# Fourteen four-quarter loads cut into 112 and 16 rows, and the early output rows written in five pieces

## The chip, the cores and the metric

The kernel runs on one core of a Trainium2 chip. The metric is the device time in microseconds of one execution; where several executions are given, the median counts. Lower is better.

## The reference

One decode step (one new token per batch entry, 8 entries, model width 448) through two layers. Each layer is attention over a long cache and then an MLP:

```python
def _A_ref(x, k_cache, v_cache, wq, wo):          # 16 query heads, 8 kv heads, 4096 keys, head width 256
    q = (x @ wq).reshape(B, 1, 16, 256) ...
    scores = einsum("bhqd,bhkd->bhqk", q, k) * 256 ** -0.5
    o = einsum("bhqk,bhkd->bhqd", softmax(scores), v)
    return o.reshape(B, 1, 16 * 256) @ wo
...
x = x + _A_ref(_layernorm(x), A_k_cache, A_v_cache, A_wq, A_wo)
x = x + _B_ref(_layernorm(x), B_w1, B_w2, B_w3, B_w4)
x = x + _A_ref(_layernorm(x), A_k_cache, A_v_cache, A_wq, A_wo)   # the same caches again
x = x + _B_ref(_layernorm(x), B_w1, B_w2, B_w3, B_w4)
```

The caches are bf16; K and V have 2 MB for each of the 64 pairs of batch entry and kv head, 256 MB together. Both layers read the same caches, but they don't fit on the chip, so most of them are read from HBM twice.

## The kernel before

**Tiles.** SBUF holds a pool `kv` of 30 slots called quarters, each 4096 bytes in all 128 partitions, 512 KB. One K or V tile of a head is four quarters: its 4096 keys are laid out as 128 rows of 32 keys, 16 KB each, so a load of a whole tile reads 128 contiguous rows of 16 KB and writes one row into each partition. Some quarters are kept from one layer's pass to the next (`KEEP_K`, `KEEP_V`), so the loads differ in size: one, two, three or four quarters.

**Order of the work.** The kernel records its operations with an engine, a duration, the keys that it reads and writes, and a priority (`Plan.op`). `Plan.schedule` then simulates all engines and fixes each engine's instruction order, and `Plan.synchronise` derives the semaphore waits. SP issues the loads in a fixed order of priority. When a load's turn comes, `next_kv` picks the free quarters, and `issue_kv` (L642 to L650) writes the DMA instruction at L648:

```python
slot_n[q] += 1
o.emit = lambda eng: eng.dma_start(dst, src)
o.dma = (slot_sem[q], 16 * slot_n[q])
```

Each quarter has a semaphore of its own, counted up by 16 per load; a reader waits for the count. Before the instruction SP waits until the last reader of the quarters, mostly a matmul (L1278, L1408), has finished. SP issues in order, so a load that waits for a quarter holds back those behind it.

**Counting TensorE's instructions.** The planner also models that TensorE's own instructions are fetched from memory in blocks of 128 matmul pairs (a weight load and a matmul): `fetched` counts them, and `pairs` in `schedule` is the number so far.

**The output.** The last results come in two parts. `with_first_results` finishes six batch entries early, in the step of entry `MLP_ROW`, and `result(6, 0)` (L1524) transposes them into `o_row`, six rows of 448 elements in six partitions, and writes them with one DMA at L1538. It is an SP instruction in the middle of the kv loads, placed by `OUT_AT`. The buffer `o_row` lies over `kh`, which later operations write again, and they wait for that DMA. The last two entries go out at the end, from L985, by SP and ACT, four rows each of `o_last`. SP's last instructions wait for the semaphores of the three writes.

The functions that the change touches:

Of the kernel before, what the change touches and what calls it, by code (L numbers as in the profile page):

```python
# [6 lines left out]
P = 128  # L7
B = 8
D = 448
# [14 lines left out]
HOLD = 2  # L24
MARGIN4, MARGIN2 = 6, 2
REP = 24
AT = (-4, -3, -2)
MLP_ROW, MLP_AT, MLP_TO = 5, 3, 7
G = D // 4
OUT_AT = 23.5  # L30
# [61 lines left out]
class Plan:  # L92
# [69 lines left out]
    def schedule(self):  # L162
# [26 lines left out]
        pairs, next_block = 32, 0.0  # L189
# [3 lines left out]
        n = 0  # L193
# [47 lines left out]
        while n < len(self.ops):  # L241
# [26 lines left out]
            if e == "sp":  # L268
                o = sp_next[sp_i]
                sp_i += 1  # L270
                if o.unit is not None:


                    _, m, q = kv_at
                    for x in range(m):
                        p = sp_next[sp_i - 1 + x]
                        p.unit.slot = q + x
                        if self.tenant[q + x] is not None:
                            o.deps[self.tenant[q + x]] = False
                        self.free_at[q + x] = 1e9  # L280
                        if x:
                            for s in p.succ:
                                del s.deps[p]
                                if o in s.deps:
                                    left[s] -= 1
                                else:
                                    s.deps[o] = True
                                    o.succ.append(s)
                            taken.add(p)
                            gone.add(p)  # L290
                            n += 1
                    sp_i += m - 1
                    self.issue_kv(o, m, q)
            else:
                while pend[e] and pend[e][0][0] <= t + 1e-9:
                    r, i, o = heapq.heappop(pend[e])
                    if o not in taken:
                        heapq.heappush(avail[e], (o.prio, i, o))
                while avail[e][0][2] in taken:
                    heapq.heappop(avail[e])  # L300
                o = heapq.heappop(avail[e])[2]
            if e == "pe" and self.filler and not quiet and t - free["pe"] > 0.1:
# [3 lines left out]
                while u + 0.22 <= t + 0.06:  # L306
# [18 lines left out]
                    while win < w:  # L325
# [5 lines left out]
                    u, pairs, next_block = self.fetched(u, f.dur[0] if warm else f.dur[1],  # L331
                                                        f.dur[3], pairs, next_block)
# [20 lines left out]
            else:  # L353
                d = o.dur
                if e == "pe":

                    w = int(t / self.WIN)
                    while win < w:
# [5 lines left out]
                    end, pairs, next_block = self.fetched(t, d[0] if warm else d[1], d[3],  # L364
                                                          pairs, next_block)
# [113 lines left out]
def bass_interleave_layers__gqa_block_cached__mixer_s_mlp__decode_kernel(  # L479
# [20 lines left out]
    plan = Plan()  # L500
# [62 lines left out]
    def over(name, shape, dt, at, skip=0):  # L563
        return nc.alloc_sbuf_tensor_at(name, shape, dt, offset=at.manual_sbuf_range[0] + skip)
# [11 lines left out]
    o_row = over("o_row", [B, D], bf, kh)  # L576
# [32 lines left out]
    s_out = nc.alloc_semaphore("s_out")  # L609
    s_outs = [nc.alloc_semaphore(f"s_out{i}") for i in range(2)]  # L610
    sems = {e: nc.alloc_semaphore(f"s_{e}") for e in ("pe", "dve", "act", "pool")}
    slot_sem = [nc.alloc_semaphore(f"s_slot{i}") for i in range(QUARTERS)]
    slot_n = [0] * QUARTERS

    def bcast(ap, shape, axis):

        dims = [list(x) for x in ap.ap]
        dims.insert(axis, [0, shape])
        return bass.AP(tensor=ap.tensor, offset=ap.offset, ap=dims)
# [19 lines left out]

    loads = [0]  # L640

    def issue_kv(o, n, q):  # L642

        (cache, b, h), u = o.unit.tile, o.unit.u
        src = cache[b, h].rearrange("(m s) d -> m (s d)", m=P)[:, u * 2048:(u + n) * 2048]
        dst = kv[:, q * 2048:(q + n) * 2048]
        slot_n[q] += 1
        o.emit = lambda eng: eng.dma_start(dst, src)  # L648
        o.dma = (slot_sem[q], 16 * slot_n[q])
        o.dur = ((n << 15) / 26.88e3 + 8 * 0.008) / FASTER + SHORT * (n < 3)  # L650

# [17 lines left out]
    KH = ["kh", ("khb", 0), ("khb", 1)]  # L669
# [18 lines left out]
    def const_c(v):  # L688
# [7 lines left out]
            wr=["sel"])  # L696
# [7 lines left out]
    for bank, key in [(psR, "R"), (psM, M)]:  # L704
        plan.op("dve", lambda v, bank=bank: v.memset(bank[:, :], 0.0), 0.5, "const",
                wr=["psM", ("row", 0), ("row", 1)], banks=[key])
# [7 lines left out]
    def dv(fn, dur=0.13, rd=(), wr=(), banks=(), name="chain", prio=None):  # L714
        if prio is None:
            prio = urge[0] + len(plan.ops)
        return plan.op("dve", fn, dur, name, rd=rd, wr=wr, banks=banks, prio=prio)
# [6 lines left out]
    def pe(fn, n, rd=(), wr=(), banks=(), name="chain", prio=None, width=20):  # L724

        if prio is None:
            prio = urge[0] + len(plan.ops)
        d = 0.06 + 0.026 * n
        return plan.op("pe", fn, (d, max(d, 0.06 + n * width / 1200), width * n, n), name, rd=rd, wr=wr, banks=banks, prio=prio)

    def mark(o):

        if where[0][1] != "psM":
            o.tbank = where[0][1][1]
# [370 lines left out]
    done = {}  # L1105
# [12 lines left out]
    def front(layer, b, h, prio=None):  # L1118
# [12 lines left out]
        def rhs(c):  # L1131
            a = at_q(layer, b, c) + 2 * h
            return qz[:, a:a + 2]
# [9 lines left out]
        def score(parts):  # L1143
            def sc(t):
                last = None
                for u, s, a in parts:
                    i = 8 * u + s


                    for c in range(2):  # L1150
                        last = t.matmul(ps[:, SB + 2 * i:SB + 2 * i + 2 * REP], a()[:, c:256:2],  # L1151
                                        bcast(rhs(c), REP, 1), start=(c == 0), stop=(c == 1))
                return last
            return sc

        def score_op(u, ss, where_of, keys):
            n = 2 * len(ss)
            return plan.op("pe", score([(u, s, lambda s=s: where_of(s)) for s in ss]),
                           (0.022 * n + 0.06, n * 2 * REP / 1200 + 0.01, n * 2 * REP, n), "sc",
                           rd=qk + keys, wr=[("sc", par, x) for x in range(u, 4)], banks=[bk],  # L1160
# [363 lines left out]
    def result(n, at):  # L1524

        ps, key, bk = where[0]

        def ot(t):
            last = None
            for kc in range(4):  # L1530
                w = P if kc < 3 else 64
                last = t.transpose(ps[0:n, :].bitcast(bf)[:, kc * P:kc * P + w],
                                   xoT[0:w, kc, at:at + n], ident_b[0:w, 0:w])
            return last
        pe(ot, 4, rd=[("xo", at), "ident_f"], wr=[key], banks=[bk])
        mark(dv(lambda v: v.tensor_copy(o_row[0:n, :], ps[0:n, :].bitcast(bf)[:, 0:D]), dur=0.5,
           rd=[key], wr=["o_row"] + KH, banks=[bk]))
        plan.op("sp", lambda eng: eng.dma_start(out[at:at + n, 0, :], o_row[0:n, :]), 0.1, "out",  # L1538
                rd=["o_row"] + KH, wr=[("done", n)],
                dma=(s_out, 16), prio=loads[0] + OUT_AT)  # L1540

    def mid(b, heads):

# [97 lines left out]

    def both(layer, b, heads, ahead=(), lag=1, AT=AT):


        tasks = []
        n = len(heads)
        for i in range(n + lag):
            if i < n:
                tasks.append(("f", layer, b, heads[i]))
            tasks += [("f",) + a for a, at in zip(ahead, AT[len(AT) - len(ahead):]) if at == i - n]  # L1650
            if i >= lag:
                tasks.append(("b", layer, b, heads[i - lag]))
        return tasks

    def with_first_results(k, b):

        if b != MLP_ROW:
            return run(k)
        run(k[:MLP_AT])
        urge[0] = 0  # L1660

        i = tcount[0] % NT
        where[0] = (psT[i], ("psT", i), ("T", i))
        held_banks.add(i)
        mlp(x3T[:, :, :], "x3all", B - 2, xoT[:, :, 0:B - 2], [("xo", 0), "x3all"])
        result(B - 2, 0)
        urge[0] = CH
        where[0] = (psM, "psM", M)
        run(k[MLP_AT:MLP_TO])
        held_banks.remove(i)  # L1670
        run(k[MLP_TO:])
# [11 lines left out]
    for b in range(B):  # L1683
# [16 lines left out]
        else:  # L1700
            k = both(1, b, l2_heads, [(1, b, h) for h in free_heads], AT=LAST_AT)
            for h, at in zip(l2_heads[-1:] + free_heads, BACKS):
# [28 lines left out]
    with nc.Block() as blk:  # L1731
        @blk.gpsimd
        def _(gp):
            plan.emit("pool", gp, sems)

        @blk.sync
        def _(eng):
            plan.emit("sp", eng, sems)
            for s in [s_out] + s_outs:
                eng.wait_ge(s, 16)  # L1740

        @blk.tensor
        def _(pe_):
            plan.emit("pe", pe_, sems)

        @blk.vector
        def _(v):
            plan.emit("dve", v, sems)

        @blk.scalar  # L1750
        def _(a):
            plan.emit("act", a, sems)
# [28 lines left out]
```

## Time and profile before

| | |
|---|---|
| time, median of 3 runs | 1073.85 us (1071.85 to 1077.86) |
| the profiled execution's own time | 1071.22 us |
| its span, first to last instruction | 1069.4 us |
| granted TensorE clock | 0.964 |
| TensorE matmul busy | 938.3 us (88%) |
| VectorE, ScalarE busy | 600.6 us (56%), 332.2 us (31%) |
| read from HBM | 434.18 MB, 406 GB/s over the span |
| kv loads of four quarters | 70 of K (22.6 us from issue to landing), 61 of V (18.5) |
| kv loads of one quarter | 168 of V (8.5 us), 26 of K (8.2) |

The page gives one profiled execution. Its slices show the busy share of each engine in tenths, and for DMA the mean busy share of the core's sixteen DMA engines. The time from issue to landing of a load includes the time that it stands in the queue behind earlier loads. The trace also has, for each DMA, one event for each part that lands, and each DMA packet with its queue, size and duration.

### The profile page before, as it was taken

The numbers are of one execution on the slowest core, as the hardware profiler recorded it, in microseconds if no ns is written. First come the engines' busy times: TensorE is split into PE (matmuls) and PEld (weight loads), VectorE is DVE, ScalarE is ACT, GpSimd is POOL, SyncE is SP. The second block draws the span as 40 slices with busy tenths as digits, with TensorE's granted clock in tenths as the row PEclk, the third lists the DMA queues.
The fourth block names the chain that finished last, engine by engine and source line by source line (L and its number), as shares of the span: only waits on it lengthen the run. The fifth ranks groups of instructions, "written<-read, shape, count | busy, mean of one in ns | idle before, by whom it ended". The sixth has DMA issues, their size and how long they took to land.

```text
span 1069.4 us, 34024 instructions
## 1 busy us (share of the span) xinstructions
PE 938.3 (88%) x15170; PEld 655.7 (61%) x15170; DVE 600.6 (56%) x1899; ACT 332.2 (31%) x926; POOL 99.6 (9%) x284
## 2 busy tenths in 40 slices
PE   5989899898989989898888878998899899898896
PEld 4556666565657656666565656766666676666664
DVE  4345455655556555565565655665555655666564
ACT  1234113341323403244132431334223432253141
POOL 0000010010100101001010100100010100111011
PEclk9899899999998999999999998999999989999997
DMA  9999999999999999999999999999999999999995
GB/s 364 408 427 423 409 398 426 427 421 400 415 424 426 421 398 410 427 425 419 395 422 425 426 410 375 426 426 424 403 400 423 425 405 379 416 423 419 373 423 235
DMA packets 56814, 436.39 MB, mean 408 GB/s; under 512 B 6094, under 2 KB 9308, under 8 KB 34652
## 3 DMA queue, kind: packets, MB, share of 16 engines
q1 hardware_dynamic: 56500, 433.84, 98.5%
q8 instruction: 119, 1.95, 0.7%
q10 hardware_dynamic: 168, 0.38, 0.1%
q14 instruction: 27, 0.22, 0.1%
HBM read 434.18 MB, written 0.01 MB: 406 GB/s over the span
## 4 chain that ended last, share of the span: by engine, by line
DMA 54%; PE 37%; DVE 6%; issue 2%; ACT 1%; SPq 0%; POOL 0%
DMA kv<-in_A_k_cache_dram 34%; DMA kv<-in_A_v_cache_dram 21%; PE psT L1512 12%; PE psP L1278 7%; PE psT L1408 4%; PE psM L1151 3%; PE psM L904 2%; PE psR L1342 2%; PE psP L1721 1%; PE psM L1068 1%; DVE oS L1306 1%; DVE oS L1304 1%; PE psM L920 1%; DVE kv L1443 1%; PE psP L1314 1%
## 5 line engine op out<-in xcount | busy, mean ns | idle before, releaser
L1512 PE MATMUL psT<-ident_f,kv 128*128 128x128 f32 x2752 | 379.5, 285 | 26.2 <-DMA kv<-in_A_k_cache_dram 24.7
L1512 PEld LDWEIGHTS psT<-ident_f,kv 128*128 128x128 f32 x2752 | 306.8, 144 | 107.7 <-issue 54.6
L1443 DVE COPY kv<-psT 128x512 f32<-128x512 f32 x384 | 262.5, 690 | 179.1 <-PE psT L1512 171.7
L1444 ACT COPY kv<-psT 128x512 f32<-128x512 f32 x336 | 195.9, 586 | 382.0 <-PE psT L1512 310.3
L1278 PE MATMUL psP<-kv,pT 128*2 128x256 bf16 x4032 | 165.4, 277 | 20.1 <-DMA kv<-in_A_v_cache_dram 16.6
L1408 PE MATMUL psT<-kv,qz 128*32 128x512 bf16 x1664 | 134.7, 397 | 6.1 <-DVE kv L1443 2.0
L1278 PEld LDWEIGHTS psP<-kv,pT 128*2 128x2 bf16 x4032 | 81.1, 82 | 59.2 <-DMA kv<-in_A_v_cache_dram 22.0
L1231 POOL PARTITION_ALL_REDUCE gm<-pm x128 | 45.4, 355 | 762.3 <-DVE pm L1229 759.8
L1241 ACT ACTIVATE pT<-sS,nb,fac 128x32 bf16<-128x32 bf16 x128 | 52.6, 417 | 123.2 <-DVE nb L1235 123.2
L1304 DVE CAST oS<-psP 128x256 bf16<-128x256 f32 x126 | 53.1, 422 | 40.6 <-PE psP L1278 39.3
L1245 POOL PARTITION_ALL_REDUCE Db<-rs x128 | 51.0, 398 | 188.9 <-ACT pT L1241 188.9
L1342 PE MATMUL psR<-wo_sb,oT 128*1 128x448 bf16 x444 | 61.0, 359 | 7.3 <-DVE oT L1321 3.5
L1314 PE MATMUL psP<-sel,oS 128*128 128x28 bf16 x504 | 32.8, 177 | 33.4 <-DVE oS L1306 30.9
L1423 DVE CAST sr<-psT 128x512 bf16<-128x512 f32 x60 | 41.5, 691 | 34.7 <-PE psT L1408 34.5
L1314 PEld LDWEIGHTS psP<-sel,oS 128*128 128x128 bf16 x504 | 23.3, 97 | 61.4 <-DVE oS L1306 57.1
L1408 PEld LDWEIGHTS psT<-kv,qz 128*32 128x32 bf16 x1664 | 34.3, 95 | 41.2 <-issue 12.3
L1241 ACT ACTIVATE pT<-sS,nb 128x32 bf16<-128x32 bf16 x128 | 40.7, 326 | 59.0 <-DVE nb L1235 59.0
L1306 DVE TENSOR_TENSOR oS<-psP,oS 128x256 bf16<-128x256 f32 x126 | 53.3, 423 | 2.9
L1721 PE MATMUL psP<-ident_f 128*128 128x256 bf16 x326 | 51.4, 283 | 0.0
L1224 DVE CAST sS<-psM 128x64 bf16<-128x64 f32 x128 | 28.1, 219 | 39.9 <-PE psM L1151 24.7
L1151 PE MATMUL psM<-qz,kv 128*128 128x48 bf16 x1344 | 45.2, 183 | 3.6 <-issue 2.1
L1151 PEld LDWEIGHTS psM<-qz,kv 128*128 128x128 bf16 x1344 | 38.9, 96 | 15.3 <-issue 5.1
(197 smaller groups left out, 805.3 us busy)
## 6 DMA issues: line engine op xcount, KB each, us to landing
kv<-in_A_k_cache_dram SPq DMA_DIRECT2D x70, 2048.0 KB, 22.6
kv<-in_A_v_cache_dram SPq DMA_DIRECT2D x61, 2048.0 KB, 18.5
kv<-in_A_v_cache_dram SPq DMA_DIRECT2D x168, 512.0 KB, 8.5
kv<-in_A_v_cache_dram SPq DMA_DIRECT2D x16, 1024.0 KB, 9.1
kv<-in_A_k_cache_dram SPq DMA_DIRECT2D x10, 1536.0 KB, 17.5
kv<-in_A_k_cache_dram SPq DMA_DIRECT2D x26, 512.0 KB, 8.2
kv<-in_A_k_cache_dram SPq DMA_DIRECT2D x8, 1024.0 KB, 9.6
kv<-in_A_v_cache_dram SPq DMA_DIRECT2D x4, 1536.0 KB, 10.0
```

Of the source, the lines that this page charges most:

```text
L1151: last = t.matmul(ps[:, SB + 2 * i:SB + 2 * i + 2 * REP], a()[:, c:256:2], bcast(rhs(c), REP, 1), start=(c == 0), stop=(c == 1))
L1241: return a.activation(pT[nr][:, :, :].rearrange("p i j -> p j i")[:, jj, :], sview[:, jj, :], ACT.Exp, bias=nb[nm][:, jj:jj + 1], scale=sc ...
L1278: last = t.matmul(ps[g4:g4 + 2, PV0:PV0 + DH], pT[nr][:, k, :], slot_ap(q, s * 256, 256), start=(i < 4), stop=(i >= 28), skip_group_check= ...
L1304: plan.op("dve", lambda v: v.tensor_copy(oS[:, 0, :], po), 0.36, "o", rd=[("pv", par, x) for x in range(4)], wr=["oS0"], banks=[bk], prio=hi)
L1306: plan.op("dve", lambda v: v.tensor_tensor(oS[:, 1, :], po, oS[:, 0, :], ALU.subtract), 0.36, "o", rd=["oS0"] + [("pv", par, x) for x in r ...
L1314: last = t.matmul(ps[:, PV1 + 2 * c:PV1 + 2 * c + 2 * ON], oS[:, w, c:DH:2], bcast(sel[:, :], ON, 1), start=(w == 0), stop=(w == 1))
L1342: last = t.matmul(psR[r:r + 1, 0:D], oT[no][:, i % 2, i // 2:i // 2 + 1], wo_sb[:, a:a + D], start=(k == 1 and i < 2), stop=(k == turn_at ...
L1408: last = t.matmul(psT[bank][32 * g:32 * g + 32, :], qz[:, a:a + 32], slot_ap(qs[g // 2], g % 2 * 1024, 1024)[:, c:1024:2], start=(half == ...
L1443: return e.tensor_copy(dst, psT[bank][:, :])
L1444: return e.copy(dst, psT[bank][:, :])
L1512: last = t.transpose(psT[bank][:, s * P:(s + 1) * P], src, ident_f[:, :])
L1721: return t.matmul(dst, ident_b, bcast(ident_b[:, 0:n // 4], 4, 1), start=True, stop=True)
```

## The change

When the planner reaches a load of four quarters, and TensorE's pairs so far have passed the next multiple of 1024, that load becomes two DMAs: rows 0 to 111, and rows 112 to 127 with the source written as eight groups of two rows. Both count on the same semaphore, and the reader waits for both. The six early output rows are written by five DMAs, cut by rows and columns, and the waits for them go from 16 to 80.

```diff
+SHARE, EVERY = 8, 1024
...
-                    self.issue_kv(o, m, q)
+                    self.issue_kv(o, m, q, pairs)
...
+    shifted = [0]
...
         slot_n[q] += 1
         o.emit = lambda eng: eng.dma_start(dst, src)
+        if n == 4 and pairs >= EVERY * (shifted[0] + 1):
+            shifted[0] += 1
+            slot_n[q] += 1
+
+            def two(eng):
+                eng.dma_start(dst[0:P - 16, :], src[0:P - 16, :]).then_inc(slot_sem[q], 16)
+                return eng.dma_start(dst[P - 16:P, :], src[P - 16:P, :].rearrange("(a m) x -> a m x", a=SHARE))
+            o.emit = two
         o.dma = (slot_sem[q], 16 * slot_n[q])
...
-        plan.op("sp", lambda eng: eng.dma_start(out[at:at + n, 0, :], o_row[0:n, :]), 0.1, "out",
-                rd=["o_row"] + KH, wr=[("done", n)],
-                dma=(s_out, 16), prio=loads[0] + OUT_AT)
+        pieces = [(0, 2, 0, 150), (2, n, 0, 150), (0, 3, 150, 298), (3, n, 150, 298), (0, n, 298, D)]
+
+        def write(eng):
+            for i, (r, r1, c, c1) in enumerate(pieces):
+                last = eng.dma_start(out[at + r:at + r1, 0, c:c1], o_row[r:r1, c:c1])
+                if i < len(pieces) - 1:
+                    last.then_inc(s_out, 16)
+            return last
+        plan.op("sp", write, 0.1, "out", rd=["o_row"] + KH, wr=[("done", n)],
+                dma=(s_out, 16 * len(pieces)), prio=loads[0] + OUT_AT)
...
-            for s in [s_out] + s_outs:
+            eng.wait_ge(s_out, 80)
+            for s in s_outs:
                 eng.wait_ge(s, 16)
```

In the built program there are 14 such pairs; the planner's order of instructions on each engine is otherwise the same.

More of the change, by code (lines that the diff above doesn't have):

```diff
@@ L640, in bass_interleave_layers__gqa_block_cached__mixer_s_mlp__decode_kernel, with issue_kv @@
     loads = [0]
-    def issue_kv(o, n, q):
+    shifted = [0]
+    def issue_kv(o, n, q, pairs):
         (cache, b, h), u = o.unit.tile, o.unit.u
```

## The prediction

> **What bounds the kernel now.** I read the clock first (0.964 granted, one core), then the page's slices and DMA queues, then the chain.
>
> ```profile
> span 1069.4 us, 34024 instructions
> ...
> DMA  9999999999999999999999999999999999999995
> GB/s 364 408 427 423 409 398 426 427 421 400 415 424 426 421 398 410 427 425 419 395 422 425 426 410 375 426 426 424 403 400 423 425 405 379 416 423 419 373 423 235
> ...
> q1 hardware_dynamic: 56500, 433.84, 98.5%
> q8 instruction: 119, 1.95, 0.7%
> ...
> DMA 54%; PE 37%; DVE 6%; issue 2%; ACT 1%; SPq 0%; POOL 0%
> ```
>
> The sixteen DMA engines are busy in every slice, SP's queue q1 alone takes 98.5% of them, and over half of the chain that ended last is transfers. TensorE is busy for 88% of the span and still waits for transfers. So a microsecond added to or taken from every DMA engine is nearly a microsecond of the end. Next, what paces the queue:
>
> ```profile
> SPq L648 <- PE psP L1278: 474.5, 139, 25.8
> SPq L648 <- PE psT L1408: 243.7, 49, 12.9
> ```
>
> SP spends 718 us in these two waits for a free quarter and then issues in bursts; a four-quarter load lands 18.5 to 22.6 us after its issue and needs 4.9 us to move, so three or four lie queued. SP's own time is no limit; the time on the DMA engines is.
>
> The last view is the rate by stretch (columns: stretch, its us, five engines' busy us, granted clock, DMA share, GB/s):
>
> ```profile
> 3.40:4.40 1.00, 0.00 (x0) 0.00 (x0) 0.07 (x1) 0.00 (x0) 0.00 (x0) 1.00 1.11 237
> 4.40:5.40 1.00, 0.29 (x6) 0.24 (x7) 0.18 (x1) 0.00 (x0) 0.00 (x0) 1.00 1.27 281
> 6.60:7.80 1.20, 0.00 (x0) 0.00 (x0) 1.06 (x9) 0.00 (x0) 0.00 (x0) 1.00 0.98 410
> 160.00:200.00 40.00, 35.80 (x472) 25.27 (x469) 22.69 (x61) 12.07 (x31) 3.01 (x8) 0.96 1.01 425
> ```
>
> From 3.4 to 5.4 us the only loads under way are those of 64 rows (wqx and w3x). All engines are busy (a share over 1 is packets side by side), yet they move 237 to 281 GB/s. The 128-row loads at 160 us move 425 with the same share. The packets say the same: a 4096-byte packet of the 64-row load has a median of 274.5 ns, a full-speed one 159. So which rows a DMA writes decides its rate, and not only how many engines share it.
>
> **Part 1: fourteen loads cut in two.** The built program of the change holds 14 pairs of a 112-row and a 16-row load of 16 KB rows; the other instructions stand in the same order on every engine. It removes nothing, and the bytes are the same.
>
> *Is work moved between DMA engines?* The design is plain: eight engines would take two of the last 16 rows each (7 + 2) and eight none (7). In this trace a load has as many landing events as it has rows where these are under 16 (eight for the 8-row x, six for the 6-row output, four for the 4-row ones) and sixteen for 128 rows. [...] But in the built program the source is one dimension of 16 rows: the step of `a` is twice the step of `m`, so the two were merged, and both sides are 16 rows of 8192 elements. I therefore expect sixteen engines with one row each, 7 + 1 = 8 as before, and nothing moved. [...]
>
> *Cost of the cut itself.* 14 more issues at about 0.4 us (1.24 us for the pair of loads at 2.88) are 5.6 us on SP, hidden behind its 718 us of waits; uncovered they would cost 0.4 us each. Behind each stands the next kv load, with the queue some 15 us deep. Semaphore packets: 14 more on each engine at 9 ns, 0.1 us.
>
> *Cost of other rows on the engines.* No 112-row and no 16-row load is in the trace; the nearest rows are the 128-row and the 64-row rate. The 112-row part (1.835 MB) takes 4.32 us at 425 GB/s and 7.74 at 237: 0 to 3.4 us more. The 16-row part (0.262 MB) takes 0.62 us at 425 and 1.11 at 237, 0.5 more; should a quarter of 64 rows mean a quarter of its rate, 4.4 us, 3.8 more. Below nothing neither can go without moved work. I take 1.1 us for the first (seven eighths of the rows are closer to 128 than to 64, but seven rows per engine no longer make equal groups of four) and 1.6 for the second, between 0.5 and 3.8, nearer to the row that exists. Together 2.7 us per load, between 0 and 7.2.
>
> 14 x 2.7 = 38 us of DMA time (0 to 101). Some is absorbed: in the eight stretches of small V loads (about 20 us each, 160 of 1069, 15%) SP's waits set the pace and not the engines, so I let 15% go: 32 us. What is late next is TensorE's transpose of the K load behind the pair (PE psT waits for in_A_k_cache_dram already).
>
> [...]
>
> **Part 2: the output in five pieces.** One issue of 0.31 us at 868.66 becomes five, so 1.2 us more on SP, and 18 packets of about 300 bytes in place of six (a 896-byte packet took 42 ns), under 0.3 us on the few engines that carry them. Behind the pieces the next kv loads wait:
>
> ```profile
> 868.66 0.31 SPq L1538 DMA_DIRECT2D out_dram<-o_row  x1
> 870.10 0.35 SPq L648 DMA_DIRECT2D kv<-in_A_v_cache_dram  x1
> 871.55 6.80 SPq L648 DMA_DIRECT2D kv<-in_A_k_cache_dram  x2
> ```
>
> The second of the loads at 871.55 waits for its quarter far longer than 1.2 us, so the delay is covered; without the cover it costs 1.2 us. The next writer of the same memory (the copy to kh at 890.1) is 16 us behind the landing at 874, and the final wait for 80 has been met since then. Nothing.
>
> **Sum.** 1071.22 us of the profiled execution (its span 1069.4 and 1.8 around it) + 32 = 1103. That execution is 2.6 us under the median of the runs, so the forecast for a median is 1073.85 + 32 = 1106.
>
> **The rivals.**
> *The work does move, and the end comes earlier* (1068). The eight engines that also carry the instruction fetches lag: at 25.2 us fifteen parts of a load land within 0.43 us and one 1.84 us after the first; at 79 us seven or eight lag by 1.5 to 2; before a stretch of small loads the spread is 4 to 5.4 us, then it shrinks because the early engines run dry. [...] A fetch of 16 KB takes 0.7% x 16 x 1069 / 119 = 1.0 us, 15 per late engine. If the 16 rows go to the eight light ones, each late engine is rid of 14 rows of 0.62 us, 8.6 us at most. The earliest engine runs dry by some 19 us in all over the eight stretches, others by less, so the light ones can take most of it before they set the end: about 6 us less. It decides if the pair's second load lands in eight parts and the unusual rows cost under 0.4 us per load. Against it stands the merged pattern. Chance 0.07.
> *Nothing moves and nothing collides*: the sixteen parts are as fast as before, because the neighbours in the queue fill the gaps. Then SP's and the packets' 0 to 2 us are all: 1075. For it: the 64-row loads are at the start, where the queue isn't yet deep. Against it: all engines were already busy there. Chance 0.15.
> *The slowest engine takes the whole blow each time.* A load counts as landed when its last part does; if the same engines share their rows' way in all 14 pairs, the delay per load is nearer to 5 us than to 2.7: 70 us, 1144. The fixed lag of the fetch engines shows that a lag persists over a whole stretch. Chance 0.15.
> *The work moves and the rows collide*: the fetch engines gain 0.6 us per pair and lose some 2, about 20 us, 1094. Chance 0.08.
>
> **The numbers.** My case (2.7 us per load, nothing moved; its own range 1084 to 1125) has the remaining 0.55. Half a per cent, 5.4 us, is about what a measurement of this kernel can tell from no change. Faster by more: the first rival, 0.07. Within it: 0.15. Slower: 0.55 + 0.15 + 0.08 = 0.78. The range must leave out no more than 2 in 10: from 1072, which drops the first rival and a little of the second, to 1136, which takes in the lower half of the third.
>
> **What would show it.** The DMA issues should list 14 groups' worth of 1792 KB and 256 KB loads. If I am right, 16 KB packets near them take longer than 614 to 621 ns, the GB/s of the slices with a pair falls from 420 to 427 to about 400, TensorE's waits for kv grow, and the spread between the parts of a load is no smaller. If the first rival holds, the spread stays near 2 us before the small loads, and the packets keep their length. The forecast is wrong if the pairs move at 420 GB/s.

## The result and the profile after

The median is 1180.18 us (6 runs, 1175.22 to 1186.70) against 1073.05 us before (6 runs): a ratio of 1.100, 95% interval 1.0955 to 1.1041. The change costs 107 us, 7.65 us for each of the 14 cut loads. The direction was forecast, the size not: the forecast was 32 us.

The page of the profiled execution (1184.59 us, its span 1182.7):

```profile
span 1182.7 us, 34042 instructions
...
PE 967.8 (82%) x15170; PEld 671.6 (57%) x15170; DVE 601.4 (51%) x1899; ACT 332.2 (28%) x926; POOL 99.6 (8%) x284
...
DMA  9999999999999999999999999999999999999995
GB/s 365 412 426 395 308 400 332 424 421 403 328 332 410 418 371 326 426 313 398 360 333 424 358 360 402 332 426 417 245 386 414 336 410 396 318 337 390 336 325 247
...
q1 hardware_dynamic: 56748, 433.84, 98.3%
...
DMA 63%; PE 30%; DVE 4%; issue 1%; SPq 1%; ACT 0%; POOL 0%
```

SP's queue moves the same 433.84 MB, and its engines are as busy as before: 98.3% of 1182.7 us is 1162.6 us per engine, where 98.5% of 1069.4 was 1053.4. The 109 us between are nearly all of the 113 us that lie between the two profiled executions (1184.59 and 1071.22 us). The DMA engines don't stand still more than before; the packets take longer. The GB/s row shows where: many slices fall to 308 to 337, one to 245, between others that stay at 424 to 426.

The stretches around one pair (issued at 169.79 and 170.16 us), columns as before, the last two DMA share and GB/s:

```profile
170.00:181.00 11.00, 10.35 (x170) 7.93 (x159) 7.45 (x23) 4.39 (x13) 1.51 (x4) 1.00 1.00 423
181.00:195.00 14.00, 7.12 (x105) 4.41 (x103) 4.44 (x12) 2.99 (x8) 0.76 (x2) 0.89 1.02 227
195.00:205.00 10.00, 8.40 (x92) 6.42 (x94) 4.77 (x11) 2.34 (x4) 0.16 (x1) 0.82 1.00 424
```

For 14 us all engines are busy and move 227 GB/s. That is 3.18 MB, more than the pair's 2.10: part of the loads ahead of and behind it goes at the slow rate as well. At 424 GB/s the same bytes take 7.5 us, so this pair costs 6.5 us. A 16 KB packet in the stretch mostly takes about 1.1 us, some up to 2.3, against 0.61 on either side; 172 of the 194 that start in it take more than 0.8 us. It isn't this pair alone: over the run 2495 of the 16 KB packets of SP's queue take more than 0.8 us, where 94 did before. That is 171 more per pair on average, and a pair has only 128.

TensorE pays (columns of the waits: us, times, longest):

```profile
PEld psT L1523 <- DMA kv<-in_A_k_cache_dram: 98.2, 60, 6.4
PE psT L1523 <- DMA kv<-in_A_k_cache_dram: 80.7, 50, 6.3
PE psP L1289 <- DMA kv<-in_A_v_cache_dram: 46.3, 33, 5.1
```

The same three waits before:

```profile
PEld psT L1512 <- DMA kv<-in_A_k_cache_dram: 42.0, 55, 5.1
PE psT L1512 <- DMA kv<-in_A_k_cache_dram: 24.7, 40, 5.0
PE psP L1278 <- DMA kv<-in_A_v_cache_dram: 16.6, 25, 1.3
```

The pairs' two DMAs stand in the list of issues (KB each, us to landing), and each has sixteen landing events (the semaphore packets of 4 bytes are 236 more than before: 16 for each of the 14 added loads, and 12 for the output's pieces):

```profile
kv<-in_A_v_cache_dram SPq DMA_DIRECT2D x8, 1792.0 KB, 16.3
kv<-in_A_k_cache_dram SPq DMA_DIRECT2D x6, 1792.0 KB, 21.8
...
kv<-in_A_v_cache_dram SPq DMA_DIRECT2D x8, 256.0 KB, 21.4
kv<-in_A_k_cache_dram SPq DMA_DIRECT2D x6, 256.0 KB, 25.4
```

### The profile page after: what moved, and what is told of

Read it like the earlier page. It is cut to its first block, busy times and chain, and to the rows that moved or that the text cites. A ratio compares the mean times of both kernels' runs of the same rounds, so it can differ in the third digit from the quotient of the medians.

```text
span 1182.7 us, 34042 instructions
## 1 busy us (share of the span) xinstructions
PE 967.8 (82%) x15170; PEld 671.6 (57%) x15170; DVE 601.4 (51%) x1899; ACT 332.2 (28%) x926; POOL 99.6 (8%) x284
## 3 DMA queue, kind: packets, MB, share of 16 engines
q1 hardware_dynamic: 56748, 433.84, 98.3%
## 4 chain that ended last, share of the span: by engine, by line
DMA 63%; PE 30%; DVE 4%; issue 1%; SPq 1%; ACT 0%; POOL 0%
DMA kv<-in_A_k_cache_dram 34%; DMA kv<-in_A_v_cache_dram 29%; PE psT L1523 11%; PE psP L1289 6%; PE psT L1419 3%; PE psM L1162 2%; PE psM L915 1%; PE psM L1079 1%; PE psR L1353 1%; DVE oS L1317 1%; DVE oS L1315 1%; PE psM L931 1%; DVE kv L1454 1%; PE psP L1739 1%; PE psP L1325 1%
## 5 line engine op out<-in xcount | busy, mean ns | idle before, releaser
L1523 PE MATMUL psT<-ident_f,kv 128*128 128x128 f32 x2752 | 394.6, 293 | 82.0 <-DMA kv<-in_A_k_cache_dram 80.7
L1523 PEld LDWEIGHTS psT<-ident_f,kv 128*128 128x128 f32 x2752 | 319.6, 149 | 166.9 <-DMA kv<-in_A_k_cache_dram 98.2
L1289 PE MATMUL psP<-kv,pT 128*2 128x256 bf16 x4032 | 168.4, 282 | 48.0 <-DMA kv<-in_A_v_cache_dram 46.3
L1419 PE MATMUL psT<-kv,qz 128*32 128x512 bf16 x1664 | 138.7, 407 | 6.3 <-DVE kv L1454 2.0
L1353 PE MATMUL psR<-wo_sb,oT 128*1 128x448 bf16 x444 | 64.2, 375 | 7.3 <-DVE oT L1332 3.5
L1739 PE MATMUL psP<-ident_f 128*128 128x256 bf16 x326 | 54.8, 297 | 0.0
```

The lines of the kernel that those rows point to most:

```text
L1289: last = t.matmul(ps[g4:g4 + 2, PV0:PV0 + DH], pT[nr][:, k, :], slot_ap(q, s * 256, 256), start=(i < 4), stop=(i >= 28), skip_group_check= ...
L1353: last = t.matmul(psR[r:r + 1, 0:D], oT[no][:, i % 2, i // 2:i // 2 + 1], wo_sb[:, a:a + D], start=(k == 1 and i < 2), stop=(k == turn_at ...
L1419: last = t.matmul(psT[bank][32 * g:32 * g + 32, :], qz[:, a:a + 32], slot_ap(qs[g // 2], g % 2 * 1024, 1024)[:, c:1024:2], start=(half == ...
L1523: last = t.transpose(psT[bank][:, s * P:(s + 1) * P], src, ident_f[:, :])
L1739: return t.matmul(dst, ident_b, bcast(ident_b[:, 0:n // 4], 4, 1), start=True, stop=True)
```

## The experiments

My theory now was *rows*: the cut loads put rows on the DMA engines in an order in which the engines hinder each other while writing. The rivals were the output pieces, the mere doubling of the DMAs, the piece's spread over all sixteen engines, and the reading side.

### Which part of the change: e1_output_only, e2_cut_only

```diff
-        if n == 4 and pairs >= EVERY * (shifted[0] + 1):
+        if False:
```

is the first; the second has the cut loads and the output's one DMA of before.

> The output goes in five pieces, no load is cut. Rows theory (the cut loads put rows on the DMA engines in an order in which the engines get in one another's way, and the whole queue falls to about 230 GB/s around each of the 14 pairs): within 0.3% of before, 1071 to 1076 us. Rival, output (the five small writes are a real part of the 107 us): 1080 us or more.

> The 14 loads are cut, the output goes in one piece as before. Rows theory: the whole loss, 1172 to 1185 us. Rival, output: under 1170 us.

Output alone: 1073.81 us, ratio 1.0019 (1.0004 to 1.0034). Cut alone: 1178.48 us, ratio 1.1005 (1.0976 to 1.1034). The loss is in the cut, but for at most 3.6 us that the five pieces may cost. Their issue in the profile of the whole change (columns: start, us) is covered as forecast, for the loads behind again wait for quarters:

```profile
957.53 1.53 SPq L1553 DMA_DIRECT2D out_dram<-o_row  x5
959.11 0.36 SPq L651 DMA_DIRECT2D kv<-in_A_v_cache_dram  x1
959.51 6.64 SPq L651 DMA_DIRECT2D kv<-in_A_k_cache_dram  x2
```

All runs from here but the one with 7 pairs have the one-piece output.

### Two DMAs, or other rows: e3_columns

```diff
-                eng.dma_start(dst[0:P - 16, :], src[0:P - 16, :]).then_inc(slot_sem[q], 16)
-                return eng.dma_start(dst[P - 16:P, :], src[P - 16:P, :].rearrange("(a m) x -> a m x", a=SHARE))
+                eng.dma_start(dst[:, 0:7168], src[:, 0:7168]).then_inc(slot_sem[q], 16)
+                return eng.dma_start(dst[:, 7168:8192], src[:, 7168:8192])
```

> The same 14 loads become two DMAs of the same sizes as in the change, 1792 and 256 KB, on the same semaphore, but cut by columns: 7168 and 1024 elements of all 128 rows. One-piece output. Rows theory: the loss is gone but for shorter packets and 14 more issues, 1073 to 1080 us. Rival, two DMAs (the second DMA, its issue or the doubled count on one semaphore costs 7 us per load): 1160 us or more.

1074.40 us, ratio 1.0022 (1.0008 to 1.0037). The same DMAs by number and size, issued in the same place, on the same semaphores, cost 2 us in all, not 106. The stretch with its second pair (issued at 159.59) shows no dip:

```profile
166.00:180.00 14.00, 11.48 (x175) 7.37 (x164) 7.02 (x20) 4.49 (x13) 1.11 (x3) 1.00 1.01 422
180.00:194.00 14.00, 11.73 (x174) 7.63 (x173) 7.80 (x21) 3.60 (x10) 1.15 (x3) 1.00 1.00 422
```

### The work moved as the change was written: e4_eight_rows

```diff
-                return eng.dma_start(dst[P - 16:P, :], src[P - 16:P, :].rearrange("(a m) x -> a m x", a=SHARE))
+                eng.dma_start(dst[112:120, :], src[112:120, :]).then_inc(slot_sem[q], 16)
+                return eng.dma_start(dst[120:128, :], src[120:128, :])
```

> The 16 rows go as two DMAs of 8 rows, so that they can reach at most eight DMA engines each: one row each on eight engines, twice, and 7 + 2 against 7 rows per engine, as the change was written. Rows theory: moving the work is worth at most 8.6 us and the rows still get in each other's way, 1150 to 1200 us. Rival, moved work (the loss comes from the piece having gone to all sixteen engines): near or under 1073 us.

1195.40 us, ratio 1.115 (1.112 to 1.117), the upper end of what *rows* expected and 17 us above the cut alone. The two 8-row DMAs land in eight parts each (224 more 4-byte packets than before, as for one 16-row DMA), so work is moved if both go to the same eight engines, which the trace doesn't name. That the piece went to sixteen engines isn't why the change is slow: this program is slower still. It also has a third DMA and eight adjacent rows at a time, so what moving the work alone does isn't separated.

### Which of the two parts: e5_112_alone

```diff
-                eng.dma_start(dst[0:P - 16, :], src[0:P - 16, :]).then_inc(slot_sem[q], 16)
-                return eng.dma_start(dst[P - 16:P, :], ...)
+                return eng.dma_start(dst[0:112, :], src[0:112, :])
```

> Of the 14 cut loads only the 112-row part is left; rows 112 to 127 of these tiles aren't loaded (stale data is used). One-piece output. It moves 3.7 MB less, 8.6 us of queue time. If the 112-row part carries the slow stretch alone: 1150 to 1170 us. If the 16-row part does: about 1064 us. If both in the measure of my prediction's terms (1.1 to 1.6): about 1105 us.

1153.57 us, ratio 1.076 (1.066 to 1.085): 82 us over before although 8.6 us less is moved, so 90 us or 6.4 us per load. Of the cut's 106 us the 16-row part, behind a 112-row part, adds the other 16, 1.2 us per load. The 112-row part makes a slow stretch without it:

```profile
178.00:189.00 11.00, 6.78 (x102) 4.13 (x99) 4.20 (x11) 2.66 (x7) 0.75 (x2) 1.00 1.01 238
```

### Another cut: e6_64_64

```diff
+                eng.dma_start(dst[0:64, :], src[0:64, :]).then_inc(slot_sem[q], 16)
+                return eng.dma_start(dst[64:128, :], src[64:128, :])
```

> The 14 loads are cut into rows 0 to 63 and 64 to 127. One-piece output. Rows theory, with the rate of the 64-row loads at the start (237 GB/s): each half takes 4.4 us for 2.5, 3.9 us more per load, and with the neighbours slowed as well up to 7: 1125 to 1170 us. Rival, part size (any row cut costs because the smaller part is short): under 1090 us.

1183.35 us, ratio 1.104 (1.095 to 1.112), 13 us above the range that I gave it: 8.0 us per load. Both parts are long, so it isn't a short part that costs. The rate is a little under that of the 64-row loads at the start of the kernel (237 to 281), and again it holds for more than the pair (13 us at 216 GB/s are 2.8 MB):

```profile
181.00:194.00 13.00, 7.17 (x94) 3.50 (x92) 3.58 (x10) 2.08 (x6) 0.76 (x2) 0.71 1.00 216
```

### Reading or writing: e7_one_row_whole, e8_one_row_cut

Both read one 16 KB row for all 128 partitions, the first in one DMA, the second cut as in the change:

```diff
+            one = bass.AP(tensor=src.tensor, offset=src.offset, ap=[[0, P]] + [list(x) for x in src.ap[1:]])
...
-                eng.dma_start(dst[0:P - 16, :], src[0:P - 16, :]).then_inc(slot_sem[q], 16)
+                eng.dma_start(dst[0:112, :], one[0:112, :]).then_inc(slot_sem[q], 16)
```

> The 14 loads stay whole, 128 rows, but all rows read one and the same 16 KB row of the cache (wrong values, same amount). It is the control for the next. If reading one row 128 times is no slower than 128 rows: 1066 to 1076 us; then the next one can be read.

> The 14 loads are cut into 112 and 16 rows as in the change, but all rows read one and the same 16 KB row (wrong values, same amount). Rows theory with the trouble on the writing side (the partitions that the engines write at the same time): as slow as the change, 1160 to 1190 us. Rival, reading side (the order in which the engines read the cache's rows): near the control, under 1090 us.

Whole: 1073.66 us, ratio 1.0019 (1.0001 to 1.0037). Cut: 1183.65 us, ratio 1.104 (1.098 to 1.110), as slow as the change. With the reads the same, the cut still takes the rate from 430 to 233 GB/s, so which rows of the cache this cut reads doesn't matter. What is left is the writing side, the partitions that are written at the same time:

```profile
166.00:180.00 14.00, 12.67 (x210) 9.31 (x207) 8.16 (x27) 5.71 (x18) 1.90 (x5) 1.00 1.02 430
180.00:194.00 14.00, 8.31 (x103) 4.59 (x101) 4.45 (x11) 2.80 (x8) 0.76 (x2) 0.85 1.02 233
```

### The sum over pairs: e9_every_2048

```diff
-SHARE, EVERY = 8, 1024
+SHARE, EVERY = 8, 2048
```

> The change with every 2048 instead of 1024 pairs, so 7 cut loads for 14, output in five pieces. If each pair costs its 7 to 8 us by itself: half the loss, 1120 to 1132 us. If the cost is a lag that the first pairs bring and later ones add nothing to: above 1145 us.

1127.81 us, ratio 1.052 (1.048 to 1.056): 56 us for 7 pairs, 8.0 each. Each pair costs about the same by itself; no lasting lag is needed to explain the loss.

### Which rows at the same time: e10_apart, e11_adjacent, e12_apart_upper

Each loads the first 4096 columns of all rows in one DMA, and then eight DMAs of 8 rows for the other 4096 columns of half of the rows (those columns of the other half are left out):

```diff
+                last = eng.dma_start(dst[:, 0:4096], src[:, 0:4096])
+                for j in range(8):
+                    last.then_inc(slot_sem[q], 16)
+                    rows = slice(32 * (j // 4) + j % 4, 32 * (j // 4) + 32, 4)   # e10: 0, 4, ... 28; ...
+                    rows = slice(8 * j, 8 * j + 8)                               # e11
+                    rows = slice(64 + 32 * (j // 4) + j % 4, 64 + 32 * (j // 4) + 32, 4)   # e12
+                    last = eng.dma_start(dst[rows, 4096:8192], src[rows, 4096:8192])
```

(one of the three lines for `rows` in each).

> The 14 loads keep their 128 rows for the first half of the columns; the second half is loaded for rows 0 to 63 only (the rest is left out), in eight DMAs of 8 rows, each of rows four apart (0, 4, ... 28 and so on). [...] Rival, any DMA with fewer than 128 rows costs: 1130 us or more.

> The same as the run with rows four apart, the same number and sizes of DMAs and the same part left out, but each of the eight DMAs has 8 adjacent rows (0 to 7, 8 to 15, and so on). [...] Rival, any DMA with fewer than 128 rows costs: as slow as the run with rows four apart.

> As the run with rows four apart, but the eight DMAs load rows 64 to 127 (64, 68, ... 92 and so on) and those of 0 to 63 are left out. If only the engines of one DMA get in each other's way: as the first, 1062 to 1085 us. If they also meet the engines that write these partitions in the whole loads beside them: between the two, 1085 to 1150 us.

Four apart in the lower half: 1076.21 us, ratio 1.0036 (1.002 to 1.005). Adjacent: 1112.22 us, 1.037 (1.032 to 1.043). Four apart in the upper half: 1135.30 us, 1.059 (1.052 to 1.066). The stretch with the second cut load, in the same order; the last is that of the eight small DMAs and the loads beside them:

```profile
171.00:186.00 15.00, 13.47 (x158) 9.35 (x156) 7.89 (x19) 5.86 (x16) 1.16 (x3) 1.00 1.01 424
```

```profile
178.00:187.00 9.00, 5.85 (x93) 3.23 (x91) 3.30 (x10) 2.07 (x6) 0.75 (x2) 0.97 1.01 309
```

```profile
176.00:187.00 11.00, 4.67 (x82) 2.75 (x80) 2.98 (x9) 1.49 (x5) 0.76 (x2) 0.89 1.03 239
```

The number of DMAs, their row counts and bytes are the same in all three; which rows are loaded, and so which partitions are written, differs, and that makes 4, 40 or 63 us against before, 36 and 59 us between the first and the others. SP's issue isn't behind it: the eight small DMAs of the second cut load take 5.34 us to issue in the first and third run and 2.70 in the second.

In the first run hardly any packet is lengthened (an 8 KB packet in the stretch takes 0.31 to 0.32 us, half of a 16 KB one, and over the run 235 of the 16 KB packets take more than 0.8 us, 213 before, instruction fetches included), so fewer than 128 rows need not slow the queue. That it ends 4 us later than before although it moves 7.3 MB less, 17 us of queue time at 424 GB/s, isn't explained by a run; each small DMA has eight landing events (896 more packets under 512 B than before, 14 x 8 x 8), and if these are the same eight engines each time, they carry as much as before. Adjacent rows at one time do lengthen the packets (8 KB: median 0.50 us in the stretch). The upper run (0.62 us, and 1.21 for the 16 KB packets) shows that a DMA can be hindered by, and hinder, the whole loads beside it: its own eight rows are as far apart as in the first.

What the runs show is that the partitions written at the same time decide the rate: 424, 309 and 239 GB/s in the three stretches. Why these rows hinder each other and those don't isn't shown: the trace names no DMA engine, so neither which engines carry the small DMAs nor which rows of a 112-row part each engine takes can be read from it.

## Why the prediction was wrong

**The bound was right.** A microsecond on every DMA engine is nearly a microsecond at the end: 109 us of longer packets, 113 us between the two profiled executions.

**Nothing moved: right.** The 16-row DMA has sixteen landing events. That puts out both rivals in which the work moves to eight engines (1068, and 1094 with collisions); e4_eight_rows, with its 16 rows in parts of eight, took 1195. The rival in which nothing collides (1075) is out as well: the packets are longer.

**Issue, semaphores, output: right.** e3_columns puts two DMAs for one at 2 us for all 14 loads, e1_output_only the five pieces at about 0.2%.

**The cost of other rows: wrong, and it is the term that failed.** I took 1.1 us for the 112-row part, "seven eighths of the rows are closer to 128 than to 64". It costs 6.4 us. For the 16-row part I took 1.6; it adds 1.2. Two errors are in the first. Nearness in row count was no measure: the stretch with the 112 rows goes at 238 GB/s, as slow as the stretch of the 64-row loads (237 to 281). And I charged the low rate to the part's own bytes alone, which made 3.4 us the upper end, while the slow stretch takes in the loads ahead and behind; I had put their part at nothing and given no reason. That equal groups of four rows per engine, my other ground for the 1.1, count for anything is shown by no run; what the runs showed in its place is the 6.4. That the two upper ends together, 7.2 us, lie just under the 7.65 that were measured is luck: they are 3.4 and 3.8, where the runs have 6.4 and 1.2. The sign that I named, slices with a pair at about 400 GB/s, came out at 308 to 337.

**The row that I went by was misread.** I took the stretch from 3.4 to 5.4 us as that of 64-row loads alone. It isn't: six 16 KB packets of the first whole K load start between 5.05 and 5.43 us, beside SP's last 64-row load, and take 1.02 to 1.32 us, where packets from 6.3 us on take about 0.61. So the trace of before already held a whole load at half speed beside a load of fewer rows. Nor does a 64-row load always have long packets: the 274.5 ns are those of SP's load, while ACT's, of the other 64 partitions, has a median of 159 ns (from 2 to 3 us, at a DMA share of 0.54 and 209 GB/s).

**The 15% absorbed: wrong.** In the profiled executions 7.8 us per load are lost in the queue (109 / 14) and 8.1 reach the end (113 / 14). Nothing was absorbed.

**The rival of 70 us** came nearest in size, but its mechanism (the slowest engine lags while the others go on) isn't what the trace shows: 172 of 194 packets in the slow stretch are long, far more than those of a few engines, and the queue's time grew by 109 us per engine on average.

## What to carry to other kernels

Where a kernel is bound by its DMA queue, keep loads at 128 rows and cut them by columns; the same two DMAs cost 2 us cut by columns and 106 us cut by rows. If rows must be cut, price the neighbours in the queue too: around one pair the low rate held for 3.2 MB, half as much again as the pair's 2.1. Row cuts aren't always dear: eight rows four apart in the lower half of the partitions lengthened hardly any packet (235 of 16 KB over 0.8 us in the run, 213 before). When a cost is bounded by a row of another shape, ask what the two shapes share before interpolating by size.

## What was not expected of the hardware

- The stretch around a 112-row DMA of 16 KB rows runs at 238 GB/s (2.6 MB in 11 us, where the DMA has 1.8), 128 rows at 424: the loads beside it are drawn down with it.
- Eight DMAs of 8 rows four apart in partitions 0 to 31 and 32 to 63 run beside full loads at 424 GB/s; the same in partitions 64 to 127 at 239.
- Reading one 16 KB row 128 times is as fast as reading 128 rows (ratio 1.0019).
- TensorE's granted clock is lower in the slower runs: 0.927 over the profiled run of the change against 0.964, with the mean transpose matmul at 293 ns for 285. It isn't low in every slow stretch (0.89 in that of the change and 0.82 after it, 0.71 with 64 and 64 rows, but 1.00 with the 112-row part alone). The 109 us that the queue itself takes longer leave little of the loss to the clock.
